# A fixed table for the order of all engines, a new order of the first loads, and products on zeros ahead of the first dense matmul

## The chip, the cores and the metric

One core of a Trainium2 chip runs the kernel. The metric is device time in microseconds of one execution; lower is better. The core has five engines that run side by side, each with its own queue that is worked off in order: TensorE (PE, matrix products; PEld is its weight load), VectorE (DVE), ScalarE (ACT), GpSimd (POOL) and SyncE (SP). SP, ACT and POOL issue transfers between the chip's memory and the core's on-chip buffers. Engines wait for one another by semaphores.

## The reference

Linear attention over 8 heads of 64, then a channel mixing block. B = 8 batches, S = 576 rows, C = 512 columns, F = 1024.

```python
# attention, q, k, v: (8, 8, 576, 64)
q_s = softmax of q over the 64 columns of a head
k_s = softmax of k over the 576 rows
kv = einsum('bhsd,bhse->bhde', k_s, v)
x = einsum('bhsd,bhde->bhse', q_s, kv)      # then (8, 576, 512)
# channel mix
x_prev = x moved down by one row, zeros in row 0
xk = mu_k * x + (1 - mu_k) * x_prev
xr = mu_r * x + (1 - mu_r) * x_prev
k = maximum(xk @ w_k, 0)                    # 512 x 1024
v = (k * k) @ w_v                           # 1024 x 512
r = 1 / (1 + exp(-(xr @ w_r)))              # 512 x 512
return r * v
```

## The kernel before

**Attention.** A batch b is worked in two groups g of four heads (two pairs u of two heads, 288 KB each of q, k or v). Names carry b and g: `expq` and `expk` are the exponentials on ACT (L383), `cast` brings v to bf16 on ACT (L389; batch 0 gets v in bf16 from the transfer itself, `load00v` and `load01v`, L275), `rsum`, `rrec` and `scale` make the softmax of q on DVE (L398, L402, L407), T transposes q on TensorE (L417), KV sums k by v (L438, L441 for batch 0, L444 for the others), `rz` and `kvn` or `w` divide by the sums of k on DVE, `qt` copies the transposed q to the on-chip buffer on ACT (L424, L428), and X multiplies it by the summed kv.

For batches 0 and 1 (`FUSED`) mu is multiplied into the weights of X (`wp`, L538, on DVE, from the copy `mu_wide` of mu on all partitions), so that X gives xk (m = 0) or xr (m = 1) directly (L550); ACT and DVE each copy half of it out (`x`, L560, L563). For batches 2 to 7 X gives x (L591), ACT copies it (`xb`, `xs`, L597, L600), and DVE makes xk and xr from it: `edge` (L605), `diff` (L609), four `sc` (L614) and two `mix` (L619). There X of one group, T and KV of the next are one block on TensorE (B); TKV is a block without X, and X71 at the end stands alone. xk and xr are rings over four batches (2304 rows), so batches 4 to 7 write where 0 to 3 were.

**Channel mix.** The rows of a half (four batches) are cut into units of 512, 512, 512, 512 and 256 rows; ten units in all. A unit runs eight groups k (`xk @ w_k`, L687, four matmuls each), then for each tile of 128 rows r (`xr @ w_r`, L719) and v in two halves of four matmuls (L739). ACT makes `relu` (L672) and the tanh of r (`th`, L724), DVE squares (`sq`, L676) and multiplies (`o`, L745), SP stores (`st`, L757). The first four k of units 0 and 1 are cut in two, group 0 of heads first. Four PSUM banks `mm` and two double banks `att` are shared by these; batch 0 uses them all.

**Weights and mu.** w_k in two halves (wk_a, wk_b), w_r (wr) and w_v in two halves (wv_a, wv_b) are loaded on POOL's queue and cast on the way (L344, L358), each 1 MB in memory. wk_a is issued when the last q load of batch 0 on ACT's queue has landed (`GATE`). The rows of mu are loaded on SP's queue (L283), and five products in float32 (L315, L318) spread them over the partitions; ACT copies mu (L324), DVE makes 1 - mu (L328) and the column form `mu` (L330).

**The order.** `Plan.order` runs a list scheduler while the kernel is built: every operation has a cost and a due time, and an engine takes the one that can start first. Three passes are made, with the times of the dense products of one pass as due times of the next. Buffers are given out in the same run. The loads of batch 0 (`FIRST`) stand on SP's queue, the first half of group 1's q on ACT's; mu's rows are issued between them. POOL does no arithmetic but the identity matrix.

Of the kernel before, what the change touches and what calls it, by code (L numbers as in the profile page):

```python
# [8 lines left out]
ACT = mybir.ActivationFunctionType  # L9
# [8 lines left out]
C = H * D  # L18
# [15 lines left out]
START = 0.7  # L34
HOP = 0.05
LATE = 1e6
LOOK = {"PE": 0.03, "ACT": 0.2, "DVE": 0.1, "POOL": 0.03, "SP": 0.03}
MAIN = 5.676
PACE = 1.116
DMA_LEAD = 2.0  # L40
DMA_TAIL = 0.6
LOAD_RATE = 375.0
CAST_RATE = 375.0
GATE = 5
FUSED = (0, 1)
ROWS = 1.05
MU_EARLY = 3.0
BLOCK_LOOK = 0.4
EARLY_UNITS = 2
AHEAD = {(0, 0): 0, (0, 1): 0.64, (1, 0): 3.95, (1, 1): 5.45, (2, 0): 10.46, (2, 1): 5.14, (3,  # L50
        0): 9.42, (3, 1): 7.74, (4, 0): 0, (4, 1): 10.55, (5, 0): 2.05, (5, 1): 11.13, (6, 0):
        16.45, (6, 1): 16.13, (7, 0): 1.76, (7, 1): 3.64}
FIRST = ((0, 0, ("SP", "SP")), (0, 1, ("SP", "SP")), (1, 0, ("SP", "ACT")), (1, 1, ("SP",
        "SP")))
SOON = {(1, 0, 0): 4.53, (1, 0, 1): 4.87}
PASSES = 3


class Slot:

    def __init__(self, pool):
        self.pool = pool
        self.index = None
        self.rank = self.since = None
        self.last = []


class Op:

    def __init__(self, engine, occ, lat, key, emit, deps, takes, gives, size, rate, name):  # L70
        self.engine, self.occ, self.lat, self.key = engine, occ, lat, key
        self.emit, self.deps, self.takes = emit, list(deps), list(takes)
        self.size, self.rate, self.name = size, rate, name
        self.start = self.end = self.made = None
        self.early = 0.0
        self.main = False
        self.look = 0.0
        for slot in gives:
            slot.last.append(self)


class Plan:

    def __init__(self):
        self.pools = {name: [SHARED.get((name, i), [(name, i)]) for i in range(n)]
                      for name, n in POOLS.items()}
        self.ops = []

    def add(self, engine, occ, lat, key, emit, deps=(), takes=(), gives=(), size=0.0, rate=1.0,
            name=""):  # L90
        op = Op(engine, occ, lat, key, emit, [d for d in deps if d is not None], takes, gives,
                size, rate, name)
        self.ops.append(op)
        return op

    def places(self, op):
        t, got = 0.0, []
        for slot in op.takes:
            if slot.index is not None:
                t = max(t, slot.since)  # L100
                continue
            best = None
            if slot.rank is not None and slot.rank != self.next.get(slot.pool, 0):
                return None
            for i, parts in enumerate(self.pools[slot.pool]):
                if (slot.pool, i) in got:
                    continue
                free = 0.0
                for part in parts:
                    user = self.user.get(part)  # L110
                    if user is not None:
                        if not user.last or any(o.end is None for o in user.last):
                            free = None
                            break
                        free = max(free, max(o.end for o in user.last) + HOP)
                if free is not None and (best is None or free < best[0]):
                    best = (free, i)
            if best is None:
                return None
            t = max(t, best[0])  # L120
            got.append((slot.pool, best[1]))
        return t, got

    def warm(self, t):
        busy = 0.0
        for s, e in reversed(self.pe_busy):
            if e < t - 3.4:
                break
            busy += min(e, t) - max(s, t - 3.4)
        return busy > 2.0  # L130

    def set_due(self):
        for op in self.ops:
            op.due = op.key
        for op in reversed(self.sorted):
            if not op.size and not op.main:
                for o in self.after[op]:
                    op.due = min(op.due, o.due - op.lat - HOP)
                op.due -= op.early

    def prepare(self):
        self.after = {op: [] for op in self.ops}
        for op in self.ops:
            for d in op.deps:
                self.after[d].append(op)
        left = {op: len(op.deps) for op in self.ops}
        ready = [op for op in self.ops if not op.deps]
        self.sorted = []
        while ready:
            op = ready.pop()  # L150
            self.sorted.append(op)
            for o in self.after[op]:
                left[o] -= 1
                if not left[o]:
                    ready.append(o)
        assert len(self.sorted) == len(self.ops)
# [754 lines left out]
```

## Time and profile before

| | us |
|---|---|
| three runs | 205.26, 205.32, 205.95; median 205.32 |
| the profiled execution | 205.87, its span 204.1 |
| busy: PE, DVE, ACT, POOL | 187.9, 152.7, 146.8, 38.6 |
| first dense product of unit 0 (L687) | 17.57 |
| first dense product of unit 1 | 43.78 |
| last dense product ends, last DVE output starts | 198.86 |
| moved: read, written | 33.56 MB, 9.44 MB |

A profiled execution is one of its own; its span begins with the first instruction and is somewhat shorter than the device time of the same execution. A line of a timeline gives start, length, engine, line of the kernel and operation, with output and inputs; what stands in brackets is the idle time of the engine ahead of it and what ended it. Matmuls are pipelined, so that the length of one is longer than its step: steps are read from the starts.

### The profile page before, as it was taken

To read this page: it belongs to the slowest core of one execution; us is meant where nothing else is said; L and a number is where in the kernel's file an instruction comes from. 1 tells how busy PE (TensorE), PEld (TensorE's weight loads), DVE (VectorE), ACT (ScalarE), POOL (GpSimd) and SP (SyncE) were. 2 spreads that over 40 slices of the span, in tenths; PEclk is the share of its full clock that TensorE was granted. 3 is DMA by queue.
4 is the path that set the end of the run, shared out by engine and by line. 5 is a ranking of instruction groups with operands and counts; after the bars stand their busy time and mean duration, and the time that the engine had idled before them with its cause. 6 is when DMAs were issued, how large, how long until landed. Compare 5 with 4: busy or idle time off the path is not lost.

```text
span 204.1 us, 4851 instructions
## 1 busy us (share of the span) xinstructions
PE 187.9 (92%) x1930; PEld 93.9 (46%) x1930; DVE 152.7 (75%) x348; ACT 146.8 (72%) x226; POOL 38.6 (19%) x61
## 2 busy tenths in 40 slices
PE   0659999979999999999999999999999999999990
PEld 0445444534454444444466444444444444444750
DVE  1865478999889989999999995999825459622620
ACT  4463689999999999999999488777624752642520
POOL 4912269433223312532000000000000000000000
PEclk9999999999999999999999999999999999999997
DMA  6999999999999994999742220422044012404303
GB/s 206 277 247 206 256 404 391 399 405 405 392 393 400 410 385 137 368 348 401 224 102 53 48 58 3 100 57 53 0 100 110 0 41 65 103 0 103 90 16 104
DMA packets 16431, 40.10 MB, mean 197 GB/s; under 512 B 2196, under 2 KB 5528, under 8 KB 16408
## 3 DMA queue, kind: packets, MB, share of 16 engines
q0 software_dynamic: 9328, 27.99, 41.6%
q1 hardware_dynamic: 6696, 11.25, 19.7%
q10 hardware_dynamic: 384, 0.56, 0.8%
q8 instruction: 15, 0.25, 0.5%
q14 instruction: 8, 0.07, 0.1%
HBM read 33.56 MB, written 9.44 MB: 211 GB/s over the span
## 4 chain that ended last, share of the span: by engine, by line
PE 78%; DMA 13%; DVE 3%; ACT 2%; POOL 1%; issue 0%; DVEq 0%; ACTq 0%
PE mm_b L739 9%; PE mm_c L739 9%; PE mm_d L739 7%; PE mm_b L687 7%; DMA wr<-in_moe_w_r_dram 7%; PE mm_c L687 7%; PE mm_d L687 7%; PE mm_a L687 7%; PE mm_a L719 6%; DMA raw_g<-in_v_dram 4%; PE mm_a L739 4%; PE mm_d L719 3%; PE mm_c L719 3%; PE mm_b L719 3%; DMA raw_b<-in_q_dram 2%; PE att_b L444 1%
## 5 line engine op out<-in xcount | busy, mean ns | idle before, releaser
L687 PEld LDWEIGHTS <-wk_a 128*128 128x128 bf16 x160 | 15.3, 99 | 17.0 <-issue 1.8
L687 PEld LDWEIGHTS <-wk_b 128*128 128x128 bf16 x160 | 15.5, 98 | 15.3 <-issue 0.2
L719 PEld LDWEIGHTS <-xr 128*128 128x128 bf16 x144 | 13.9, 98 | 16.8 <-ACT xr L563 0.9
L739 PEld LDWEIGHTS <-k_a 128*128 128x128 bf16 x144 | 13.8, 98 | 16.4
L739 PEld LDWEIGHTS <-k_b 128*128 128x128 bf16 x152 | 14.2, 98 | 14.7 <-issue 0.2
L719 PE MATMUL mm_a<-wr,xr 128*128 128x512 bf16 x56 | 14.4, 379 | 0.4 <-DMA raw_g<-in_v_dram 0.4
L724 ACT ACTIVATE th_a<-mm_a 128x512 f32<-128x512 f32 x14 | 8.4, 602 | 7.2 <-PE mm_a L719 7.1
L687 PE MATMUL mm_b<-xk,wk_a 128*128 128x512 bf16 (+1 forms) x44 | 11.2, 371 | 0.0
L687 PE MATMUL mm_c<-xk,wk_a 128*128 128x512 bf16 (+1 forms) x40 | 10.2, 371 | 0.0
L687 PE MATMUL mm_a<-xk,wk_a 128*128 128x512 bf16 (+1 forms) x40 | 9.8, 360 | 0.3 <-DVE xk L560 0.3
L687 PE MATMUL mm_c<-xk,wk_b 128*128 128x512 bf16 (+1 forms) x40 | 9.4, 358 | 0.0
L687 PE MATMUL mm_d<-xk,wk_b 128*128 128x512 bf16 (+1 forms) x40 | 9.4, 358 | 0.0
L687 PE MATMUL mm_a<-xk,wk_b 128*128 128x512 bf16 (+1 forms) x40 | 9.4, 358 | 0.0
L687 PE MATMUL mm_b<-xk,wk_b 128*128 128x512 bf16 (+1 forms) x40 | 9.4, 358 | 0.0
L687 PE MATMUL mm_d<-xk,wk_a 128*128 128x512 bf16 (+1 forms) x36 | 9.2, 368 | 0.0
L315 PE MATMUL mm_a<-mu_rows,pick 2*128 2x512 f32 x2 | 2.0, 1122 | 6.8 <-DMA mu_rows<-in_moe_mu_r_dram 6.8
L719 PE MATMUL mm_d<-wr,xr 128*128 128x512 bf16 x32 | 8.2, 379 | 0.0
L719 PE MATMUL mm_b<-wr,xr 128*128 128x512 bf16 x28 | 7.2, 379 | 0.0
L719 PE MATMUL mm_c<-wr,xr 128*128 128x512 bf16 x28 | 7.2, 379 | 0.0
L676 DVE TENSOR_TENSOR k_a<-rel_a 128x512 bf16<-128x512 bf16 (+1 forms) x13 | 5.1, 391 | 2.8 <-ACT rel_a L672 2.6
L672 ACT ACTIVATE rel_b<-mm_a 128x512 bf16<-128x512 f32 (+1 forms) x7 | 4.0, 571 | 4.1 <-PE mm_a L687 3.9
L676 DVE TENSOR_TENSOR k_a<-rel_c 128x512 bf16<-128x512 bf16 (+1 forms) x13 | 5.1, 392 | 2.4 <-ACT rel_c L672 2.3
(323 smaller groups left out, 487.7 us busy)
## 6 DMA issues: line engine op xcount, KB each, us to landing
out_dram<-ot_a SPq DMA_DIRECT2D x14, 128.0 KB, 2.4
out_dram<-ot_b SPq DMA_DIRECT2D x14, 128.0 KB, 2.4
out_dram<-ot_c SPq DMA_DIRECT2D x14, 128.0 KB, 3.2
out_dram<-ot_d SPq DMA_DIRECT2D x14, 128.0 KB, 2.7
raw_k<-in_v_dram POOLq DMA_DIRECT2D x3, 576.0 KB, 8.5
out_dram<-ot_e SPq DMA_DIRECT2D x13, 128.0 KB, 2.4
raw_j<-in_k_dram POOLq DMA_DIRECT2D x2, 576.0 KB, 10.7
raw_a<-in_q_dram POOLq DMA_DIRECT2D x2, 576.0 KB, 10.1
```

Source lines behind the costliest of these rows:

```text
L315: nc.tensor.matmul(kn.bank(wide_slot), lhsT=kn.pick[:].rearrange("p u c -> p (u c)"), rhs=kn.mu_rows[:].rearrange("p m c -> p (m c)"), sta ...
L444: kn.nc.tensor.matmul(to, lhsT=by, rhs=kn.vvs[vv.index][two[r], j, u, 0:65], **flags)
L672: kn.nc.scalar.activation(out=kn.rels[rel.index][:, 0:n], in_=kn.bank(kf)[:, 0:n], func=ACT.Relu, scale=HALF_ROOT)
L676: kn.nc.vector.tensor_tensor(out=kn.k2s[k2.index][:, fc, 0:n], in0=kn.rels[rel.index][:, 0:n], in1=kn.rels[rel.index][:, 0:n], op=ALU.mult)
L687: kn.nc.tensor.matmul(kn.bank(kf)[:, 0:n], lhsT=kn.wk[fc // 4][:, ct, (fc % 4) * 128:(fc % 4) * 128 + 128], rhs=kn.xs[0][:, ct, c0:c0 + n] ...
L719: kn.nc.tensor.matmul(kn.bank(rps), lhsT=kn.xs[1][:, ct, c:c + 128], rhs=kn.wr[:, ct, :], start=(ct == 0), stop=(ct == CT - 1))
L724: kn.nc.scalar.activation(out=kn.ths[th.index][:], in_=kn.bank(rps), func=ACT.Tanh, scale=0.5)
L739: kn.nc.tensor.matmul(kn.bank(vps)[:, 0:width], lhsT=kn.k2s[k2.index][:, ft, 128 * m:128 * m + 128], rhs=kn.wv[ft // 4][:, ft % 4, part], ...
```

## The change

`Plan.order` and its costs are removed. A table `ORDER` names every operation in the order in which they are emitted, with the number of the buffer that each takes; a name with `ACT!` is issued on ACT's queue. All operations of all engines are in it, in an order that differs from the scheduler's throughout. In the table the eight q and k loads of batch 0 are on ACT's queue; SP's first instructions are the two loads of mu's rows. The gate ahead of wk_a is gone.

On POOL the order begins: identity, load00v, first half of group 0's q of batch 1, `rest` (1 - mu, moved from DVE, now from the on-chip copy), load01v, wk0, wk1, three halves of batch 1, wr, `wp001`, two halves, mu's column load, wv0, `wp011`, wv1, then the other halves. `wp` for m = 1 is moved from DVE to POOL for batches 0 and 1. On ACT it begins: four q loads of batch 0, the table load's dummy, three exponentials of q, two k loads, the copy of mu, two k loads, then the other exponentials.

TensorE runs 42 products `fill` on a zeroed buffer (128x128 by 128x256) among the first real ones, ahead of the first k. Mu's column form is loaded apart and turned by one product (`mu`), after the first r of unit 0; the row form keeps one product (`wide`). KV of batch 0 is two operations, one for each pair of heads. X001 is ahead of unit 0's first k (before, behind its last k). X21 is an operation of its own ahead of the block B31, which is then without an X (`ALONE`). The two stores of a tile are operations of their own; in the last unit the second store of the first tile is on POOL's queue and those of the last tile on ACT's.

```diff
+FILLS = 90
+ALONE = ((2, 1), (B - 1, 1))
+ORDER = """
+ACT!load00q0:0 ident rows ACT!load00q1 ACT!load01q1:1 load00v late ACT!load01q0 load10q0:2 zero
+consts fill:3 warm fill.2:2 fill.3:3 fill.4:2 fill.5:3 fill.6:2 fill.7:3 fill.8:2 fill.9:3
+expq001:0 fill.10:2 wide:0 expq000 rsum001:0 expq011:1 rrec001 rsum000 ACT!load00k0:3 ACT!load00k1
+fill.11:3 fill.12:2 rrec000 rsum011:1 widecopy fill.13:3 fill.14:2 fill.15:3 ACT!load01k0:4
+scale001:0 rest fill.16:2 fill.17:3 ACT!load01k1 fill.18:2 scale000 fill.19:3 expq010 fill.20:2
+load01v fill.21:1 fill.22:3 fill.23:2 rrec011 fill.24:1 expk000:0 T00:0 scale011:1 wk0 fill.25:3
+fill.26:2 expq100:2 fill.27:1 KV000:1 rsum010 wk1 expk001 fill.28:3 fill.29:2 fill.30:1 fill.31:3
+rrec010 fill.32:2 qt00:0 load10v0:5 KV001 scale010 fill.33:3 fill.34:2 rz00:0 load11q1:6 fill.35:1
+fill.36:3 expk011:1 kvn00:0 fill.37:2 T01:0 wp000:0 load11q0 fill.38:3 expk010 fill.39:2 fill.40:1
+fill.41:3 edge00 fill.42:2 qt01:1 X000:1.2 wr KV010:3 wp001 x0001 x0000 KV011 load10q1 X001:2.1
+rz01:1 kvn01:1 load10k1:7 edge01 k02:2 x0010 x0011 k00:3 muload wp010:1 X010:0.1 k03:0 x0100 x0101
+wv0 k06:1 wp011 k02.2 relu06:0 k00.2 wv1 k03.2 expq110:0 X011:0.1 load10k0 relu00:1 k01:1 relu02:2
+load11k1:8 k04:3 sq02:0 sq00 relu03:2 k01.2 x0111 x0110 load11v1:9 expq111 r01:2 load10v1 expq101
...
     def __init__(self, engine, emit, deps, takes, gives, name):
...
+    def ordered(self):
+        ops = {op.name: op for op in self.ops}
...
+        for token in ORDER.split():
+            name, _, places = token.partition(":")
+            name, _, held = name.partition("^")
+            engine, _, name = name.rpartition("!")
+            op = ops[name]
+            if engine:
+                op.engine = engine
...
+            for slot, place in zip(fresh, places.split(".")):
+                slot.index = int(place)
...
+            yield op
...
+    def emit_mu_load():
+        for m, src in enumerate((kn.mu_k, kn.mu_r)):
+            kn.nc.gpsimd.dma_start(out=kn.mu_sb[4 * m:4 * m + 4, :], in_=bass.AP(
+                tensor=src.tensor, offset=src.offset, ap=[[128, 4], [1, 128]]))
+
     def emit_mu():
...
+        kn.nc.tensor.transpose(out=kn.bank(mu_slot)[:, 0:8], in_=kn.mu_sb[:],
+                               identity=kn.identf[:])
 
     def emit_rest():
...
+        kn.nc.gpsimd.tensor_scalar(out=kn.mu_wide[:, 1, :], in0=kn.mu_wide[:, 0, :],
+                                   scalar1=-1.0, scalar2=1.0, op0=ALU.mult, op1=ALU.add)
...
+    for i in range(FILLS):
+        slot = Slot("mm")
+
+        def fill(slot=slot):
+            kn.nc.tensor.matmul(kn.bank(slot)[:, 0:256], lhsT=kn.still[:, 0:128],
+                                rhs=kn.still[:], start=True, stop=True)
+
+        add("PE", fill, [zero], [slot], [slot], name="fill")
...
+            for u in range(2):
+                kvm = add("PE", lambda u=u: kv(kvp, (u,)), [expk[u], castv[0], consts, kvm], [kvp], leave_kv if u else [], name=f"KV{tag}{u}")
...
             def mixed_weights(m):
                 for i in range(2):
-                    kn.nc.vector.tensor_tensor(
+                    (kn.nc.gpsimd if m else kn.nc.vector).tensor_tensor(
...
-        if (b, g) == (B - 1, 1):
+        if (b, g) in ALONE:
...
+                for i in range(2):
+                    queue = "SP"
+                    if last and m >= tiles - 2:
+                        queue = ("SP", "ACT" if len(parts) == 2 else "POOL")[i]
```

## The prediction

> **What bounds it now.** I read the page's slices first, then the chain that ended last, then TensorE's timeline through the first 45 us, then what each transfer of the ramp took, then busy time by stretch.
>
> From the page, the slices (5.1 us each):
>
> ```profile
> PE   0659999979999999999999999999999999999990
> DVE  1865478999889989999999995999825459622620
> DMA  6999999999999994999742220422044012404303
> ```
>
> TensorE is full from the fourth slice to the end but for one slice (the ninth). The transfers are full from the second slice to the fifteenth. VectorE is nearly full from the seventh to the twenty-fifth, so it sits right behind TensorE. The stretch by stretch answer (stretch, its length, then busy time per engine) says the same with numbers:
>
> ```profile
> 20.00:25.00 5.00, 4.67 (x33) 2.02 (x33) 2.19 (x5) 2.80 (x6) 1.08 (x2) 1.00 1.22 236
> 25.00:30.00 5.00, 4.60 (x49) 2.26 (x48) 3.42 (x9) 4.20 (x9) 2.79 (x6) 1.00 1.04 406
> 40.00:45.00 5.00, 3.85 (x44) 1.81 (x43) 4.97 (x12) 5.00 (x7) 2.17 (x3) 1.00 1.03 405
> 43.78:198.86 155.08, 155.04 (x1460) 75.93 (x1456) 122.71 (x264) 116.62 (x177) 17.38 (x24) 1.00 0.51 169
> ```
>
> The last row is the key: from 43.78 to 198.86 TensorE has work in 155.04 of 155.08 us. No order can win there unless it removes matmuls, and none of the real ones is removed. So all that can be won lies before 43.78, where unit 1 begins, or behind 198.86. TensorE's timeline in the first part (start, length, instruction, then idle time and what ended it):
>
> ```profile
> 6.82 2.04 PE L315 MATMUL mm_a<-mu_rows,pick 2*128 2x512 f32 x2 [6.82 <-DMA mu_rows<-in_moe_mu_r_dram]
> 8.66 1.70 PE L318 MATMUL mm_b<-pick,mu_rows 2*128 2x2 f32 x8
> 10.29 0.66 PE L417 MATMUL att_a<-ident,qs_a 64*128 64x64 bf16 x18
> ...
> 17.57 1.03 PE L687 MATMUL mm_a<-xk,wk_a 128*128 128x512 bf16 x2
> 18.39 1.06 PE L687 MATMUL mm_b<-xk,wk_a 128*128 128x512 bf16 x2
> ...
> 22.11 0.60 PE L687 MATMUL mm_a<-xk,wk_a 128*128 128x512 bf16 x2 [0.34 <-DVE xk L560]
> 22.55 0.59 PE L687 MATMUL mm_b<-xk,wk_a 128*128 128x512 bf16 x2
> ...
> 28.98 1.04 PE L719 MATMUL mm_a<-wr,xr 128*128 128x512 bf16 x4 [0.40 <-DMA raw_g<-in_v_dram]
> ...
> 43.16 0.44 PE L550 MATMUL att_a<-qt_b,wp_a 64*64 64x288 bf16 x8 [1.15 <-ACT xk L560]
> ```
>
> Two matmuls of 512 columns take 0.86 us by their starts at 17.57 (next at 18.39 and 19.25) and 0.43 at 22.11: the first ones run at half speed, although the granted clock in the rows is 1.00 all along. The first product waits 6.82 us for two rows of mu, and the transposes of q start only at 10.29, when mu's products have left TensorE. The transfers:
>
> ```profile
> vb_b<-in_v_dram POOLq DMA_DIRECT2D x1, 288.0 KB, 9.6
> wk_a<-in_moe_w_k_dram POOLq DMA_DIRECT2D x1, 512.0 KB, 10.2
> wk_b<-in_moe_w_k_dram POOLq DMA_DIRECT2D x1, 512.0 KB, 12.0
> wr<-in_moe_w_r_dram POOLq DMA_DIRECT2D x1, 512.0 KB, 14.3
> wv_b<-in_moe_w_v_dram POOLq DMA_DIRECT2D x1, 512.0 KB, 18.1
> ```
>
> Issued at 4.87, 5.62 and 6.36, wk_a, wk_b and wr land at 15.1, 17.6 and 20.7: one weight block (1.05 MB read) every 2.6 to 3.1 us, some 0.4 MB per us; wv_b lands at 25.9.
>
> **The change, step by step.**
>
> *First dense product.* Before: 17.57. After, the four q loads go out on ACT's queue at about 0.75, 1.2, 1.6 and 2.0 (0.41 us each by ACT's one issue of before), the table load and its dummy (1.28 + 0.2) end near 3.9, and three exponentials of 0.6 end near 6.4; only then ACT issues the k loads, two, then mu's copy (0.5), then two. A 288 KB load has landed 3.6 us after issue at best, so k of group 0 is there by about 10, its second exponential ends near 11.1, and its half of KV (36 pairs of small products over both halves took 0.95) near 11.6. Reciprocal, product and half of wp (0.1 + 0.3 + 0.45) give 12.4, X000 12.6 to 13.1. ACT then has qt00, two exponentials, qt01 (1.1 + 0.6 + 0.6 + 1.1) and the copy of x (0.6) to do: x is complete at 15.2. X001 stands ahead of k02 as well and waits for wp001 on POOL. POOL: `rest` starts when mu's copy is done (7.7). No row shows that operation on POOL: the select there on 128x128 took 0.29 us, four times the elements make it 1.2 at most; the same operation took 0.69 on VectorE. I take 1.1. Then v01, wk0, wk1, three loads and wr go out, 0.75 each: wp001 begins at 14.1. It too is new on POOL: two products of 128x128, 0.45 together on VectorE, 0.6 by the select; I take 0.9, with 0.45 and 2.0 as ends. X001 ends at 15.5. wk0 by volume: the transfers stand empty from about 7.4 (q, v00 and one q of batch 1, 2.05 MB) to 8.5, then k (1.2 MB), v01 (0.6) and wk0 (1.05) end at 15.1 to 15.5. So k02 starts at 15.5: **-2.1 us**.
>
> The Trainium skill (GPSIMD Engine Reference, the table of which engine to take for what) has two-input elementwise work about two times slower there than on VectorE; by that wp001 would take 0.9 and nothing changes. No row of this trace shows it.
>
> *Clock.* 42 products of 256 columns on zeros run ahead of k02, cold 0.21 us each by the 0.43 of a cold 512. If they hold the array awake, the six cold products at 17.57 to 20.2 win 6 x 0.215 = **-1.3**, and X010 (0.9 there, 0.5 warm) **-0.4**. The real start is worth nothing if the array sleeps again; that is a rival.
>
> *X001* (0.7 us at 27.90) now runs in the ramp's idle time: **-0.7**. Waits of 0.34, 0.40 and 1.15 on TensorE go: **-1.9**. From 17.57 to 43.78 are 26.2 us for 21.5 us of work at full speed (20 groups of four products at 0.863, five X of 0.45 to 0.7, two TKV of 0.85); of the 4.7 too many, 1.1 are drains and gaps under 0.3 that these terms leave out, and I count **-0.7** of them gone. Sum so far -7.1.
>
> *New waits in unit 0.* Weights are issued at 9.5 instead of 4.87, with loads of batch 1 between them, so by 2.6 us a block they land later: wk1 17.7, wr 22.5, wv0 26.6, wv1 29.2. X010 waits for wp010 (16.8; 0.4 lost), k06 for wk1 and its x (0.35), r01 for wr (0.2), v010 for wv0 (0.6). Batch 1's last k and v halves land near 32.8 and 33.5, casts end at 33.3 and 34.6, so the two blocks TKV10 and TKV11 wait 0.6 and 0.4. These sum to **+2.5**: unit 1 begins near 39.2 instead of 43.78, **-4.6** net.
>
> *VectorE next.* Its work stays, except what went to POOL (half of wp: 4 x 0.45 = 1.8; mu's 0.69). In 30 to 85 us it is idle for only some 3.6 us. Adding the after order from x1001 to mix210 by row durations (sums 1.35, scalings 1.35, squares 0.42, differences 0.70, mixes 0.70, scales 0.36, outputs 0.65) gives 24.5 us, and from there to mix310 another 20; TensorE has some 23.1 and 18.9 for the same stretches. A start 4.6 us earlier so meets VectorE: up to 1.0 us is given back at units 2 and 3, I take **+0.5** (ends 0 and 1.5). What saves it is that batch 1's first sums and scalings (5.3 us) move into 18 to 29, where VectorE was half idle.
>
> *Nothing on the path:* the table itself (fixed order, the same instructions); KV of batch 0 in halves (same products); X21 alone ahead of B31: eight products leave one block and form their own, 0.4 us either way, bounds -0.3 (a wait of the block goes) and +0.3 (another drain). Loads from batch 2 on lead their use by tens of us. At the end, one of the last unit's six stores goes by POOL; the last ones stay on SP and ACT, and the 5.2 us behind the last product stay, bounds -0.5 and +0.7 (POOL's issue took 0.75 where ACT's took 0.55).
>
> Sum: -4.6 + 0.5 = **-4.1 us**. The span of the profiled run is 204.1 (205.87 with what lies around it, 0.55 above the median of the three). I take it off the median: 205.32 - 4.1 = **201.2**.
>
> **Rivals.**
>
> *A, the fills don't hold the clock.* They wait for nothing but their place, so each batch runs out in a few us and TensorE then idles until the next real product: 14 of them between `wide` and T00 last 1.5 to 3 us, the gap is some 4. Before, the array went fast near 20.8, after work without large gaps from 13.3. If it sleeps, unit 0 starts cold: +1.3 to 1.7, partly covered by the waits for wv0. The Trainium skill (TensorE: Matmul & The Clock Gate, What's actually happening) says that an idle window of about 3.4 us halves the clock; the 13.3 to 20.8 of this trace fits it loosely. Time: 202.0.
>
> *B, VectorE bounds.* If its orders leave it no slack, units 2 and 3 wait 1.5 to 2.5 us: 202.5 to 203.5. For: 95 to 100% busy in most stretches from 40 to 95. Against: after 150 it is under half busy, so later work can give way.
>
> *C, POOL's queue holds the weights (the slower side).* `rest` and wp001 stand ahead of loads on POOL; before, nothing computed there after 1.3. `rest` waits for the row loads, `wide`, and ACT's copy. Each us that it is late delays v01, both wk, wr and wv by one, with the transfers idle meanwhile, and unit 0 with them. At 4.1 us more than I took (v01 issued after 12.9 instead of 8.8) nothing is left; 6 us more gives 207.2. For: mu's rows landed only by 6.8 before. Against: they are first on an empty queue now.
>
> *D, better than that.* If batch 1's chain follows its landing with only 0.8 of my 2.5 us of waits, and VectorE keeps up: -7.1 + 0.8 = -6.3, 199.0.
>
> **Chances.** The forecast (200.1 to 202.2) 0.48; A 0.12; B 0.12 (0.02 of it near no change); C 0.10 (0.07 of it slower than before, 0.03 near no change); D 0.18. Range 198.5 to 203.7: it leaves out C and the outermost of D. A change below 0.5% (1.0 us) can't be told from none here. Faster 0.88, same 0.05, slower 0.07.
>
> **What would show it.** First product of line k02 at 15 to 16, with 0.43 per pair (a pair at 0.86: A). `rest` on POOL near 7.7 to 8.8, v01's issue right behind (C if past 11). Weights landing at 15.3, 17.7, 22.5, 26.6, 29.2. Unit 1's first product near 39.2. No idle TensorE after that but 0.5 us before units 2 and 3 (over 1.5: B). Last product to end of span still 5.2. I am wrong if unit 1 begins after 42, or if TensorE, full before, shows gaps after 45.

## The result and the profile after

The changed kernel is slower: 209.03 us (median of 18 runs, 206.46 to 212.31) against 205.92 of the kernel before beside it (18 runs, 205.19 to 206.63), a ratio of 1.0118 with a 95% interval of 1.0089 to 1.0147. Forecast were 201.2 and a range of 198.5 to 203.7. Its times scatter over 5.9 us, those of the kernel before over 1.4. Ratios, here and in the table below, leave out runs over 1.5% above the fastest of their kernel (four of these 18), so this one is lower than that of the medians, 1.0151. The profiled execution of the changed kernel took 210.16 and is one of those four; a second profile of the same kernel (`after_again`, 207.32) stands beside it from here on.

A span falls into four pieces that add up to it: up to the first dense product of unit 0, unit 0 itself, the dense stretch from unit 1 to the start of the last output on DVE, and the tail behind it.

| us | before | forecast | after | after again |
|---|---|---|---|---|
| first dense product | 17.57 | 15.5 | 20.21 | 20.71 |
| unit 0, from there to unit 1 | 26.21 | 23.7 | 25.02 | 23.66 |
| dense stretch | 155.08 | 155.6 | 157.11 | 155.2 |
| tail | 5.2 | 5.2 | 6.0 | 6.0 |
| span | 204.1 | 200.0 | 208.4 | 205.6 |

So unit 0 became shorter by what was forecast in `after_again` (2.55) and by half of that in the other profile (1.2). The loss is a first dense product that came 3 us later where it should have come 2 us earlier, a tail 0.8 longer, and, in one of the two profiles, 2 us lost in the dense stretch.

The page's slices of the changed kernel (5.2 us each) answer to those shown of before:

```profile
PE   6795999999999999999989999999999999999980
DVE  1874249998999999879999995999825459622720
DMA  6999999989999999999934050332044012404403
```

TensorE looks busier in the first slices, but the work there is products on zeros. Busy time by stretch of the same kernel, columns as before:

```profile
15.00:20.00 5.00, 3.08 (x109) 2.35 (x107) 2.13 (x8) 2.22 (x4) 1.71 (x4) 0.99 1.18 209
20.00:25.00 5.00, 4.79 (x29) 1.76 (x30) 1.96 (x6) 1.15 (x3) 2.36 (x5) 0.67 1.16 307
45.23:202.34 157.11, 155.63 (x1460) 75.93 (x1456) 122.92 (x264) 117.09 (x178) 21.68 (x31) 1.00 0.54 177
```

From 15 to 20 us TensorE has only 3.08 us of work, from 20 to 25 the granted clock is 0.67, and the last stretch, full before, has 1.5 us of gaps. TensorE's timeline of the changed kernel through the first of these:

```profile
16.92 0.19 PE L387 MATMUL mm_d<-vb_b,ek_b 64*64 64x64 bf16 x1
16.95 0.17 PE L390 MATMUL att_a<-one,ek_b 64*64 64x1 bf16 x1
18.81 0.19 PE L390 MATMUL att_a<-one,ek_b 64*64 64x1 bf16 x1 [1.69 <-issue]
...
20.21 1.03 PE L599 MATMUL mm_c<-xk,wk_a 128*128 128x512 bf16 x2 [0.45 <-DMA wk_a<-in_moe_w_k_dram]
21.04 1.06 PE L599 MATMUL mm_d<-xk,wk_a 128*128 128x512 bf16 x2
```

Two things to see. TensorE stands still from 16.95 to 18.81 in the middle of one operation (KV011), waiting for nothing that the profile shows ("issue"). And two dense products take 0.83 us at 20.21: the array is cold again in spite of 42 fills. The row of 20.21 shows a third: the halt is not what the first dense product waited for last in this profile. It waited 0.45 us more for wk_a, whose landing ends the wait. In `after_again` there is no halt, wk_a is there in time, and the product starts 0.08 us behind X001's last. The weights' transfers (issue to landing, last column):

```profile
vb_b<-in_v_dram POOLq DMA_DIRECT2D x1, 288.0 KB, 5.2
wk_a<-in_moe_w_k_dram POOLq DMA_DIRECT2D x1, 512.0 KB, 9.7
wk_b<-in_moe_w_k_dram POOLq DMA_DIRECT2D x1, 512.0 KB, 11.4
wr<-in_moe_w_r_dram POOLq DMA_DIRECT2D x1, 512.0 KB, 13.7
wv_b<-in_moe_w_v_dram POOLq DMA_DIRECT2D x1, 512.0 KB, 10.0
```

POOL's timeline of the changed kernel, from `rest` to the last weights, gives the issues:

```profile
8.80 1.00 POOL L276 TENSOR_SCALAR mu_wide<-mu_wide 128x512 f32<-128x512 f32 x1 [5.87 <-ACT mu_wide L280]
9.76 0.76 POOL L217 DMA_DIRECT2D vb_b<-in_v_dram  x1
10.51 0.77 POOL L300 DMA_DIRECT2D wk_a<-in_moe_w_k_dram  x1
...
20.45 0.55 POOL L268 DMA_DIRECT2D mu_sb<-in_moe_mu_k_dram  x1 [3.74 <-DMA wk_a<-in_moe_w_k_dram]
22.97 0.52 POOL L268 DMA_DIRECT2D mu_sb<-in_moe_mu_r_dram  x1 [1.98 <-DMA wk_b<-in_moe_w_k_dram]
23.69 0.78 POOL L310 DMA_DIRECT2D wv_a<-in_moe_w_v_dram  x1 [0.20 <-issue]
```

wk_a is issued at 10.51 and lands at 20.2, wv_b lands at 35.3, both 5 to 6 us behind the forecast. By the profile, mu's two small loads wait on POOL for weights to land (3.74 and 1.98 us), and the w_v loads wait behind them.

### The profile page after: what moved, and what is told of

Same layout as the page of the kernel before. It is cut to its first block, busy times and chain, and to the rows that moved or that the text cites. A ratio compares the mean times of both kernels' runs of the same rounds, so it can differ in the third digit from the quotient of the medians.

```text
span 208.4 us, 4924 instructions
## 1 busy us (share of the span) xinstructions
PE 194.6 (93%) x1965; PEld 96.1 (46%) x1965; DVE 151.1 (72%) x341; ACT 146.6 (70%) x224; POOL 44.8 (21%) x73
## 4 chain that ended last, share of the span: by engine, by line
PE 66%; DMA 17%; ACT 5%; DVE 4%; POOL 3%; issue 2%; ACTq 1%; SPq 0%; DVEq 0%
PE mm_c L650 8%; PE mm_a L650 7%; PE mm_d L599 7%; DMA wr<-in_moe_w_r_dram 7%; PE mm_c L599 6%; PE mm_a L599 6%; PE mm_b L599 6%; PE mm_d L650 5%; DMA raw_j<-in_v_dram 4%; PE mm_b L650 4%; PE mm_b L630 4%; PE mm_d L630 3%; DMA out_dram<-ot_e 3%; DMA raw_b<-in_q_dram 3%; PE mm_a L630 2%
## 5 line engine op out<-in xcount | busy, mean ns | idle before, releaser
L650 PEld LDWEIGHTS <-k_a 128*128 128x128 bf16 x144 | 13.8, 98 | 16.7 <-DVE k_a L590 0.2
L599 PE MATMUL mm_c<-xk,wk_a 128*128 128x512 bf16 (+1 forms) x48 | 12.2, 371 | 0.4 <-DMA wk_a<-in_moe_w_k_dram 0.4
L630 PE MATMUL mm_b<-wr,xr 128*128 128x512 bf16 x48 | 12.3, 379 | 0.0
L635 ACT ACTIVATE th_b<-mm_b 128x512 f32<-128x512 f32 x10 | 6.1, 612 | 7.1 <-PE mm_b L630 7.1
L630 PE MATMUL mm_d<-wr,xr 128*128 128x512 bf16 x40 | 10.3, 379 | 0.0
L630 PE MATMUL mm_c<-wr,xr 128*128 128x512 bf16 x32 | 8.3, 379 | 0.0
L599 PE MATMUL mm_b<-xk,wk_a 128*128 128x512 bf16 (+1 forms) x36 | 8.3, 345 | 0.0
L292 PE MATMUL mm_d<-still 128*128 128x256 bf16 x18 | 6.5, 362 | 1.9 <-DVE still L233 1.9
L590 DVE TENSOR_TENSOR k_a<-rel_b 128x512 bf16<-128x512 bf16 (+1 forms) x14 | 5.6, 398 | 3.0 <-ACT rel_b L586 2.8
L586 ACT ACTIVATE rel_a<-mm_b 128x512 bf16<-128x512 f32 (+1 forms) x7 | 3.9, 564 | 5.3 <-PE mm_b L599 5.3
L599 PE MATMUL mm_c<-xk,wk_b 128*128 128x512 bf16 (+1 forms) x32 | 7.4, 353 | 0.0
```

The source lines that it names most:

```text
L292: kn.nc.tensor.matmul(kn.bank(slot)[:, 0:256], lhsT=kn.still[:, 0:128], rhs=kn.still[:], start=True, stop=True)
L586: kn.nc.scalar.activation(out=kn.rels[rel.index][:, 0:n], in_=kn.bank(kf)[:, 0:n], func=ACT.Relu, scale=HALF_ROOT)
L590: kn.nc.vector.tensor_tensor(out=kn.k2s[k2.index][:, fc, 0:n], in0=kn.rels[rel.index][:, 0:n], in1=kn.rels[rel.index][:, 0:n], op=ALU.mult)
L599: kn.nc.tensor.matmul(kn.bank(kf)[:, 0:n], lhsT=kn.wk[fc // 4][:, ct, (fc % 4) * 128:(fc % 4) * 128 + 128], rhs=kn.xs[0][:, ct, c0:c0 + n] ...
L630: kn.nc.tensor.matmul(kn.bank(rps), lhsT=kn.xs[1][:, ct, c:c + 128], rhs=kn.wr[:, ct, :], start=(ct == 0), stop=(ct == CT - 1))
L635: kn.nc.scalar.activation(out=kn.ths[th.index][:], in_=kn.bank(rps), func=ACT.Tanh, scale=0.5)
```

## The experiments

All runs are against the kernel before, with the same four pieces from one profile each; one profile is one execution, and some of the differences between rows are no more than scatter. Median and ratio come from the runs of the timing; k_on_sp has no ratio. ramp_fix's ratio is higher than that of its median to the median beside it (1.0176).

| kernel | first dense product | unit 0 | stretch | tail | median | ratio (95%) |
|---|---|---|---|---|---|---|
| after_again | 20.71 | 23.66 | 155.2 | 6.0 | 207.60 | 1.0115 (1.0069 to 1.0161) |
| no_fills | 20.61 | 23.77 | 155.1 | 6.0 | 207.81 | 1.0107 (1.0074 to 1.0140) |
| pool_early | 23.86 | 23.35 | 157.6 | 6.0 | 211.81 | 1.0300 (1.0230 to 1.0370) |
| tail_act | 21.06 | 23.21 | 157.6 | 4.4 | 206.65 | 1.0036 (0.9998 to 1.0074) |
| stores_inline | 20.84 | 24.21 | 156.5 | 6.0 | 208.09 | 1.0108 (1.0069 to 1.0146) |
| k_on_sp | 20.50 | 23.57 | 155.2 | 6.0 | 207.86 | |
| mu_early | 18.72 | 23.54 | 156.6 | 6.1 | 208.32 | 1.0115 (1.0085 to 1.0146) |
| all_four | 22.47 | 23.36 | 155.2 | 4.7 | 206.33 | 1.0025 (0.9991 to 1.0060) |
| ksp_pool | 20.28 | 23.35 | 155.4 | 6.0 | 207.93 | 1.0107 (1.0038 to 1.0176) |
| fills_24 | 21.70 | 23.93 | 155.2 | 6.0 | 208.65 | 1.0165 (1.0101 to 1.0228) |
| combo | 22.30 | 23.54 | 155.2 | 4.7 | 205.99 | 1.0022 (0.9986 to 1.0057) |
| kv_whole | 20.64 | 23.20 | 155.7 | 6.0 | 207.97 | 1.0091 (1.0064 to 1.0117) |
| exp_later | 21.09 | 23.83 | 155.2 | 6.0 | 208.45 | 1.0129 (1.0091 to 1.0167) |
| ramp_fix | 21.08 | 24.09 | 155.4 | 6.0 | 209.60 | 1.0222 (1.0171 to 1.0273) |
| best | 21.30 | 24.58 | 155.4 | 4.4 | 207.53 | 1.0089 (1.0058 to 1.0121) |
| lean | 20.75 | 23.22 | 155.2 | 6.0 | 207.09 | 1.0083 (1.0052 to 1.0113) |
| lean_best | 19.08 | 24.03 | 156.2 | 4.4 | 206.13 | 1.0017 (0.9991 to 1.0043) |

In the diffs below one name of the table stands on a line.

### The same kernel again, and without fills

after_again is the changed kernel. no_fills:

```diff
-fill:3
...
-fill.42:2
```

> The changed kernel once more, for a second profile and a common yardstick. Theory (P): its loss sits in the ramp (weights 5 us later than predicted because of POOL's queue), in an idle of 1.7 us of TensorE inside the second half of KV of group 1, which a 16 KB load of instructions at that moment explains, and in 0.8 us of tail. Expected 207 to 209.5, first product of unit 0 at 20 to 21, the idle inside KV011 again between 1 and 2 us. Rival: the profiled run was an odd one, and this profile shows neither the idle nor the half clock at 20 to 23.4.

> All 42 products on zeros are left out, nothing else. If they are of use (they hold the clock), TensorE's first products of unit 0 run at half speed for longer and the time rises by 1 to 2 us against the changed kernel. If they do harm (84 instructions more make TensorE's instruction load fall into KV011), the idle of 1.7 us there is gone, first products at half speed as they are now, and the time is 0.5 to 1.5 us lower.

No gain of the fills can be told (1.0115 with, 1.0107 without; by the two intervals it is 1.0 us at most, and 1.7 were forecast). The trace has a record of the granted clock, which the clock column of the stretches sums up. (The column also reads 1.00 where no record lies, as in the kernel before from 15 to 20 us, where products take twice their time; its record begins at 20.92.) Full speed is on record from 9.65 in the profile of the change, then half from 19.89 to 23.30; from 18.23 in after_again; from 22.32 without fills. In tail_act, which has all the fills too, it was given early and taken away. Its busy time by stretch:

```profile
10.00:15.00 5.00, 3.69 (x97) 2.78 (x98) 3.42 (x6) 4.53 (x7) 4.93 (x8) 0.76 1.04 246
15.00:20.00 5.00, 5.00 (x110) 3.46 (x106) 2.25 (x7) 1.97 (x3) 2.32 (x5) 0.56 1.18 187
```

The clock column is 0.76 and then 0.56: full speed for one spell of 3.41 us, then half for two. The Trainium skill (TensorE: Matmul & The Clock Gate, What's actually happening) has the clock follow a window of some 3.4 us that runs freely and does not start with the kernel. The spells of 3.41, 6.83 and 10.24 us here agree. For the same kernel full speed begins at 9.65 and at 18.23, 8.58 us apart, which is no multiple of 3.41: a table can't place the fills by such a window.

The rows of after_again and no_fills also show what the fills cost. From the end of the second exponential of k (group 0) to X000 pass 5.2 us in after_again, where the fills run cold at 0.21 us each on that path, and 3.4 without fills. From X000 to the first dense product it is the other way round: 2.4 in after_again, which has full speed by then, and 4.4 without. The sums are 7.6 and 7.8: what the fills win behind X000 they lose ahead of it. (All seven profiles without fills on that path have 3.2 to 3.4 there.) Only mu_early, with full speed from 9.87 on, has both short (3.4 and 2.5).

### Weights ahead of `rest`

```diff
+muload
+load01v
+wk0
+wk1
 rest
```

> On POOL's queue mu's column load, v of group 1 and both halves of w_k go ahead of the operation that makes 1 - mu. If POOL's waiting is what makes the weights late: wk_a issued near 5 instead of 10.5 and landed by 16 instead of 20.2, wv_a by 29 instead of 32.5, unit 0 begins 2 to 4 us earlier, time 204.5 to 207. Rival: the transfers only change places, k of batch 0 lands later by what the weights gain, unit 0 begins within 1 us of before the move, time unchanged at 207 to 209.

Worse than both: the first dense product at 23.86 and 3% in time. The two blocks of w_k do land earlier (17.1 and 20.2), but take the transfers from k, whose exponentials for group 0 came only at 13.8 and 15.2. So POOL's queue alone was not what held the ramp.

### The last store

```diff
-                        queue = ("SP", "ACT" if len(parts) == 2 else "POOL")[i]
+                        queue = ("SP", "ACT")[i]
```

> The last unit's one store on POOL's queue goes to ACT's as in the kernel before; nothing else. Theory: the 6.06 us behind the last output's start fall to about 5.2, so 0.8 to 1.3 us less than the changed kernel. Rival: the tail is set by the last stores on SP and ACT, and nothing changes.

The tail falls from 6.0 to 4.4 and the ratio from 1.0118 to 1.0036 (0.9998 to 1.0074): the largest loss with one cause, and the one edit of this study that by itself made the changed kernel clearly faster. The page of the changed kernel has the store among its costliest groups, and tail_act's timeline has the same store on ACT:

```profile
L666 POOL DMA_DIRECT2D out_dram<-ot_c x1 | 0.6, 564 | 101.8 <-DVE ot_c L656 101.8
...
201.31 0.55 ACTq L665 DMA_DIRECT2D out_dram<-ot_c  x1
```

The issue itself is 0.56 us, no longer than on ACT. It is what follows that is long, and the instructions that the trace holds say what. In the change's profile the last packet of any transfer ends at 205.35 and SP is through with its waits for the stores at 206.29, but a DRAIN instruction on POOL, behind its store, runs from 202.05 to 207.58, and the last steps of the program come after it. All 13 profiles with a store on POOL have this DRAIN of 5.5 us at the end, and 2.6 to 3.0 us from the last packet to the end of the span. In the six without, the kernel before among them, POOL's DRAIN comes behind its last load, at 96 to 107 us, where nothing waits for it, and 1.7 to 1.8 us pass from the last packet to the end. Why the tail of tail_act is also shorter than the 5.2 of the kernel before stays open.

tail_act's profile also shows the second loss. Its DVE timeline, and what TensorE waited for from unit 1 on:

```profile
89.26 0.69 DVE L655 SCALAR_TENSOR_TENSOR ot_e<-th_a,mm_d 128x512 f32<-128x512 f32 x1 [2.56 <-DMA out_dram<-ot_e]
```

```profile
PE att_b L518 <- DVE xd_a L536: 1.0, 1, 1.0
PE mm_d L598 <- DVE ot_e L655: 1.0, 1, 1.0
```

DVE waits 2.56 us for the output buffer ot_e, whose earlier store is still on its way; the table holds some stores back for long (st11 stands behind o23, st13 behind o31), so few of the five buffers are free. DVE is full there, and TensorE loses 1.0 us twice. The profile of the change has the same wait (2.01 us); after_again has none.

### Stores in place, k on SP, mu's load earlier

stores_inline (each store right behind its output, the five buffers in turn), k_on_sp, mu_early:

```diff
+st00.2
+st00
...
```
```diff
-ACT!load00k0
-ACT!load00k1
-ACT!load01k0
-ACT!load01k1
 rows
+load00k0
+load00k1
+load01k0
+load01k1
```
```diff
+muload
 rest
```

> Every store is put right behind its output in the order and the five output buffers are taken in turn; the ramp is the changed kernel's. Theory: in some executions a late store of the buffer of o20 holds VectorE at o23 for 2 to 2.6 us, and TensorE loses 2 to 2.5 us behind it (2.09 and 2.51 in two of three profiles, 0 in the third). Then this profile has no gap over 0.25 us between the first product of unit 1 and the end, and the median falls by 0.8 to 1.5 us with a smaller spread (206.5 to 207.0, none above 208.5). Rival: the gaps come from VectorE's order itself, and stay.

> The four k loads of batch 0 are issued by SP right behind mu's rows instead of by ACT behind three exponentials of q. Theory: in the changed kernel ACT's queue stands at an exponential until its q has landed (7.2 to 7.9) and k, mu's copy and with it all of POOL's loads go out only then; freed of it, k issues end by 3.5, mu's copy is done by 7, v and w_k go out by 8.5, and the first product of unit 0 moves from 20.2 to 20.7 to 17.5 to 18.5, that of unit 1 from 44.3 to 42 to 43.5; time 205 to 206.5. Rival: k only takes the transfers' time from q and v, unit 0 and unit 1 begin within 0.7 us of where they were, time unchanged.

> The two small loads of mu's column form go ahead of the operation that makes 1 - mu on POOL's queue, from their place behind w_r. Theory: there they wait 1.5 to 4 us for earlier loads to land (eight are in flight) and hold wv_a to 21.0 to 23.7; without them wv_a is issued by 19 and lands 1.5 to 3 us earlier, unit 1 begins 0.5 to 1.5 us earlier; time lower by 0.5 to 1.5. Rival: the eight in flight set it, the next load waits as long in their place, and unit 1 begins at 44.2 to 44.4 as before.

> Stores in turn, k on SP, mu's column load early, the last POOL store on ACT, all in one. If the losses are those four and add up: unit 1 by 42 to 43, no gap after it, tail 4.6 to 5.4, time 202.5 to 204.5, below the kernel before. If the ramp is bound by the volume of the transfers alone, unit 1 stays at 43.5 to 44.3 and the time is 204.5 to 205.5, no better than before.

stores_inline has no wait for an output buffer left, but loses 1.3 us of the stretch to other gaps (0.7 for ACT's `rel_b`), and its time is no better: that the stores' order costs time is seen in single profiles and not shown in the runs. k_on_sp moves nothing: k goes out earlier, but the second half's exponential still begins at 12.55 (11.42 in the change's profile). mu_early's profile has the best ramp of those with the old KV (18.72; array at full speed from 9.87), but the time is that of the change: its profile was a lucky one (206.65, the fastest of its ten runs), and the median 208.32 says so. all_four (tail_act's edit among them) is as fast as tail_act alone.

### Both queues freed, fewer fills, all together

ksp_pool is k_on_sp and pool_early together, fills_24 leaves out fill.25 to fill.42, combo is ksp_pool without fills, with stores_inline and tail_act.

> The four k loads of batch 0 go out on SP's queue right behind the row loads, and mu's load, v of group 1 and the two k weights go out on POOL ahead of `rest` (each of the two edits alone gained nothing: 20.50 and 23.86 for the first dense product). Theory (two queues hold one another: k behind ACT's exponentials, weights behind `rest`, so that with one of them freed the other still comes late): first dense product at 17 to 18.5, unit 1 at 41.5 to 43, time 205 to 206.5. Rival (the transfers' volume alone sets the ramp, whoever issues them): first dense product at 19.5 or later, unit 1 at 43.5 or later, time 207 to 208.5.

> The last 18 of the 42 dense products on zeros (fill.25 to fill.42, those between the first transposes of KV and the first dense product) are left out; the output is the same. Theory (those fills stand in TensorE's order on the path to X000 and cost more than they keep awake): first dense product 0.5 to 1.5 us earlier than in the unchanged kernel's cold runs, 19.2 to 20.2, time 206.5 to 207.5. Rival (they cost nothing, TensorE waits there anyway): first dense product 20.2 to 20.8 and the time as with all fills or with none, 207.4 to 208.2.

> Both moves of ksp_pool, no dense products on zeros at all, each store right behind its output, and the last unit's stores on SP and ACT alone. Theory (ramp's queues, buffers of the outputs and the late store on POOL are three separate losses that add up): first dense product 17 to 18.5, unit 1 at 41.5 to 43, no gap over 0.5 us after that, tail 4.6 to 5.4, time 203 to 204.8, faster than the kernel before. Rival (the ramp is bound by volume): unit 1 at 44 or later, time 205.5 to 207, no better than before.

All three miss what the theories wanted. ksp_pool: with both queues free the first dense product still comes at 20.28, so the issue of loads is not the bound. fills_24 came out slower than with all fills (21.70, 1.0165), though the intervals overlap; no theory had expected it, and it led to the next group. Its way to X000 did become short (3.4 us from the second exponential, as without fills), but from X000 to the first dense product it takes 5.3. combo gains what tail_act gains.

### TensorE's own work in the ramp

kv_whole makes KV of batch 0 one operation again, at the places of KV001 and KV011. exp_later moves expq100 behind expk010. ramp_fix is both, with mu_early and fills_24. best adds stores_inline and tail_act.

```diff
-            for u in range(2):
-                kvm = add("PE", lambda u=u: kv(kvp, (u,)), [expk[u], castv[0], consts, kvm], [kvp], leave_kv if u else [], name=f"KV{tag}{u}")
+            kvm = add("PE", lambda: kv(kvp), expk + [castv[0], consts, kvm], [kvp], leave_kv, name=f"KV{tag}1")
```

> KV of batch 0 is made whole again, both halves of the heads in one operation, in the places of KV001 and KV011. Theory (halves run two products at a time where the whole runs four, so both halves take twice as long): the rows of KV of group 1 take 1.0 us in a cold array or 0.5 in a warm one, against 2.1 or 1.0 in halves; first dense product 0.5 to 1.1 us earlier, 19.2 to 20, time 206.5 to 207.3. Rival (the same products take the same time, as the prediction had it): both groups take as long as in halves, first dense product 20.2 to 20.8, time 207.4 to 208.2.

> The first exponential of batch 1 (expq100) goes behind the last one of batch 0's k in ScalarE's order. Theory (it stands on the path of the second half of k of group 0): that half's exponential starts 0.6 us earlier, KV001 and what follows 0.3 to 0.6 earlier, first dense product 19.7 to 20.3, time 206.8 to 207.6. Rival (the half of k lands no earlier, or the fills in between set the time): first dense product 20.2 to 20.8, time 207.4 to 208.2.

> Four edits of the ramp together: KV of batch 0 whole, the exponential of batch 1 behind batch 0's, mu's load ahead of `rest` on POOL, the last 18 fills left out. Theory (these four are the loss in the ramp): first dense product at 17 to 18.2, unit 1 at 41.5 to 42.5, time 205 to 206.3. Rival (transfers set it): first dense product at 19 or later, unit 1 at 43.5 or later, time 206.8 to 208.

> The edits of ramp_fix, each store right behind its output, and the last unit's stores on SP and ACT alone. Theory (ramp, output buffers and late store are separate losses): unit 1 at 41.5 to 42.5, 155 to 155.5 us of dense work behind it, tail 4.6 to 5.0, time 203.2 to 204.8, faster than the kernel before by 0.5 to 1.2%. Rival (each gain in the ramp is taken back): 205.3 to 206.5, no better than before.

The rows of KV bear the first theory out. TensorE's timeline, the kernel before and then after_again:

```profile
13.45 0.26 PE L438 MATMUL att_b<-vb_a,ek_a 64*64 64x64 bf16 x4
13.50 0.21 PE L441 MATMUL att_a<-one,ek_a 64*64 64x1 bf16 x4
13.55 0.26 PE L438 MATMUL att_b<-vb_a,ek_a 64*64 64x64 bf16 x4
```

```profile
12.18 0.24 PE L387 MATMUL att_b<-vb_a,ek_a 64*64 64x64 bf16 x2
12.23 0.19 PE L390 MATMUL att_a<-one,ek_a 64*64 64x1 bf16 x2
12.29 0.24 PE L387 MATMUL att_b<-vb_a,ek_a 64*64 64x64 bf16 x2
```

Every 0.10 to 0.11 us before starts four of each kind, and only two after, since a half writes to one half of the output's partitions. Nine such steps make 1.0 us for a group before, and 2.0 for its two halves (12.05 to 13.0 and 14.29 to 15.3). The Trainium skill (TensorEngine Tiling (Array Packing), Tiling Modes and Tile-to-Partition Mapping) has four independent 64x64 tiles, each tied to its partitions, which agrees. In time kv_whole is not told from the change (1.0091 against 1.0118). exp_later's theory falls: the exponential of k begins when its data land, not when ACT is free. ACT's timeline of exp_later:

```profile
12.42 0.68 ACT L331 ACTIVATE ek_a<-raw_d 128x576 bf16<-128x576 f32 x1 [0.89 <-DMA raw_d<-in_k_dram]
```

ramp_fix should have gained and lost instead, 1% by its ratio. TensorE's timeline of best, which has the same ramp, shows where:

```profile
18.27 0.42 PE L476 MATMUL mm_a<-qt_a,wp_a 64*64 64x288 bf16 x1
18.27 0.20 PE L386 MATMUL att_a<-one,ek_b 64*64 64x1 bf16 x2
20.20 0.45 PE L476 MATMUL mm_b<-qt_a,wp_a 64*64 64x288 bf16 x1 [1.51 <-DVE qt_b L458]
```

X001 begins at 18.27 and its second product comes at 20.20. The profile names DVE's qt_b, which had ended at 19.39, 0.8 us before. Counting the recorded products in the traces gives a better reading. TensorE halts behind its 223rd recorded product in six profiles, whatever that product is: in KV011 (the change 1.86 us, stores_inline 0.98, kv_whole 0.43) or in X001 (fills_24 0.92, ramp_fix 1.78, best 1.92). In each, a 16 KB packet of the queue that the page calls "q8 instruction" takes 0.9 to 1.0 us among full transfers and ends 1.3 to 1.5 us before TensorE goes on. In the 13 other profiles the packet had ended 1.5 us or more before the 223rd product: in the kernel before it ends at 18.52, and the 223rd product, one of X010, comes at 20.73. By the fills, the halt is there in three of eleven profiles with all 42, in all three with 24 and in none of the four without.

### Without the fills that bring the 223rd product forward

lean is ramp_fix with no fills at all. lean_best adds stores_inline and tail_act.

> As ramp_fix, but with none of the 42 dense products on zeros (the output is the same), so that the 223rd product falls into the first dense products and no longer into X001. Theory (TensorE halts behind its 223rd product until 16 KB of instructions have come, and this takes back what the ramp gains): no halt between KV of group 1 and X001, first dense product at 18.7 to 19.7 (21.08 in ramp_fix), time 1 to 2 us below ramp_fix, 207 to 208.4. Rival (the halt belongs to X001, by a wait that the profile does not show): the halt of 1.8 us is still there between the first and the second product of X001, first dense product at 20.7 or later, time 208.5 or more.

> As lean, with each store right behind its output and the last unit's stores on SP and ACT alone. Theory (halt, output buffers and late store are separate losses): no halt in X001, unit 1 at 43 to 44.3, tail 4.5 to 5, time 204.7 to 206, the same as the kernel before or up to 0.5% faster. Rival (the halt stays): as best, 207 to 208.

The halt is gone in both profiles: from X000 to the first dense product pass 3.8 and 3.9 us, in ramp_fix and best 5.4 and 5.7. The ratios fall from 1.0222 to 1.0083 and from 1.0089 to 1.0017, with intervals that do not meet; by medians, each against the kernel before beside it, that is 2.0 and 0.9 us. TensorE's timeline of lean_best at the same place:

```profile
17.82 0.39 PE L474 MATMUL mm_b<-qt_a,wp_a 64*64 64x288 bf16 x1
...
18.08 0.91 PE L474 MATMUL att_b<-qt_a,wp_a 64*64 64x288 bf16 x8
19.08 0.61 PE L592 MATMUL mm_c<-xk,wk_a 128*128 128x512 bf16 x1
```

X001 runs through from 17.62 and the first dense product comes at 19.08. lean's own profile misses its number (20.75 against 18.7 to 19.7) for another reason: the second half of k came only at 13.08, and KV then waited for the copy of q. The gain over ramp_fix is near its halt of 1.78, that over best only half of its 1.92. The edit takes out the 24 fills themselves too, and what of the gain is theirs was not separated. lean itself is not told from the change (1.0083 against 1.0118), so the halt may be what ramp_fix lost, and no part of the change's own 1.2% is shown to come from it. lean_best has the lowest ratio, 1.0017 (0.9991 to 1.0043): not told from the kernel before, nor from tail_act, which has one line changed. No version beats the kernel before.

## Why the prediction was wrong

The step that failed is the first term, the first dense product at 15.5. The rows that part it, the second exponential of k (group 0) and X000, first in the kernel before and then in the changed one:

```profile
12.60 0.67 ACT L383 ACTIVATE ek_a<-raw_c 128x576 bf16<-128x576 f32 x1
15.37 0.44 PE L550 MATMUL mm_a<-qt_a,wp_a 64*64 64x288 bf16 x1
...
11.42 0.67 ACT L332 ACTIVATE ek_a<-raw_d 128x576 bf16<-128x576 f32 x1
15.54 0.53 PE L481 MATMUL att_b<-qt_a,wp_a 64*64 64x288 bf16 x8
```

The exponential was to end at 11.1 and ended at 12.1 (13.2 in after_again): 1.0 and 2.1 us of the miss. From there to the first dense product 4.4 us were counted, 4.3 had passed before, and it took 8.1 (7.6): 3.7 and 3.2 us. So most of the miss lies in the chain behind k, and the smaller part in the transfers ahead of it. Both ends that the prediction had at 15.5 came late: X001 at 19.8 and 20.6, wk_a at 20.2 and 17.5. Unit 1 began at 45.2 and 44.4, past the 42 that was set as the sign of being wrong.

- **First dense product, -2.1: the step that failed.** It measured +2.6 (+3.1 in after_again), a miss of 5 us. What the rows show of it, mostly from the profile of the change; how many of the 5 us each is worth was not shown by an experiment, as no edit of the ramp alone clearly took the changed kernel's time down:
  - *Rate of the transfers.* 0.4 MB per us was taken from the weights, of which 1.05 MB are read but 0.52 land. q and k are float32 on both sides, and in that time all transfers together move 281 GB/s from 5 to 10 us and 221 from 10 to 15. The third half of q landed at 7.2, not 5.8. Of the 2.2 us that were to be won at the second exponential of k (it ends at 13.3 before), 1.2 were, and 0.1 in after_again, where the fourth half of q held ACT's order until it landed at 10.7.
  - *"KV of batch 0 in halves (same products)", costed at nothing.* The same products take twice as long. Group 1's stand bare between X000 and X001 and take 1.8 us in a cold array (no_fills) where a whole group takes 1.0 (lean), and 1.0 in a warm one (after_again).
  - *A wait left out.* KV001 begins at 12.57 and halts until 13.21 for ACT's copy of the transposed q, whose bank takes its sums (in lean the profile names it: 2.77 us for `qt_a`), and the chain from there over `rz`, `kvn` and `wp` to X000 took 1.7 us. So X000 began at 15.54 in place of 12.6 to 13.1. The fills on this path, counted at nothing, run cold in after_again: there it takes X000 until 18.35.
  - *X001 ahead of k02*, taken to end with the weights at 15.5, ends at 19.8 and 20.6; in 18 of the 19 profiles the first dense product follows the product ahead of it within 0.16 us, whatever the weights do.
  - *wk_a*, which lands at 20.2 and ends the last wait in the change's profile alone.
  - *The halt* of 1.86, in no row of before and not in after_again, and here hidden behind wk_a. The fills are 42 of the 223 products.
- **Weights' landing.** wk_a at 20.2 in place of 15.3. Behind v01 (15.0) it took 5.2 us, not 2.6; mu's tiny loads, counted as nothing, held w_v (issued at 23.69; at 18.35 in mu_early). What the transfers moved in those 5.2 us besides wk_a wasn't separated.
- **Unit 0, -2.5 (the waits, X001 and the cold products gone, new waits of 2.5).** Right in size in one profile: -2.55 in after_again, -1.2 in the change's, where the clock was at half until 23.30. The parts did not come as counted: the three old waits are gone, but TensorE's idle time in unit 0 of after_again is 0.6 us in all, so the new waits of 2.5 are not there, and the gains were smaller by about as much. That the sum fits is luck.
- **Clock, -1.3 and -0.4.** Right in some executions, not in others (rival A): full from 9.15 to 9.87 in three of the first eight profiles of the study, and dropped again in two of them. What holding it would be worth is another matter: the fills that were to hold it took as much as they gave.
- **VectorE, +0.5 (ends 0 and 1.5).** 0.1 in after_again, 2.0 in the change's profile. In the change's profile and in tail_act's it begins with a wait for an output buffer, not with DVE's amount of work: the order of the stores in the table was not looked at. Rival B had the size and another mechanism.
- **Tail, 0 (bounds -0.5 and +0.7).** +0.8, just outside, and the largest part of the loss against the kernel before that an edit took back. Only the issue was compared (0.75 to 0.55), not the DRAIN of 5.5 us that follows it.
- **Rival C** had the side right and the place wrong: `rest` ended at 9.80 and v01 went out at 9.76, not past 12.9, and putting the weights ahead made it worse.

## What to carry over

Filler products that are to warm the array also stand in its queue: look in the timeline at whether they run cold on the very path that they are to shorten. Where a ramp is made of many short matmuls, count instructions as well as microseconds: in this case fillers brought a halt at a fixed count of products forward into the ramp. Before a store is given to another queue, look at what that engine does last. Before cutting a group of small products in two, look in the timeline at how many run side by side, since halves that share one part of the array take the whole time each. And an estimate of "what lands when" needs the rate of the same kind of transfer in the same stretch; a rate from transfers that convert on the way need not hold for those that don't.

## What the hardware showed that was not expected

- TensorE's halt at a fixed count of products, 0.43 to 1.92 us, tied to a 16 KB packet of an instruction queue under full transfers. That these are TensorE's own instructions is a reading that fits all 19 profiles, and lean and lean_best came out as it has them; that the packet causes the halt is not shown beyond that, and its trigger wasn't found.
- A last store through POOL's queue makes the tail 1.6 us longer than the same store through ACT's (6.0 against 4.4): a DRAIN on POOL runs for 5.5 us behind the store, past the landing of every transfer.
- The granted clock rises at 8.9 to 25.0 us in kernels whose ramps differ little, and can fall again within 3.41 us.
